# Folding a convolution's second transform stage into 64 by 64 products on sums and differences

## The chip, the cores and the metric

The kernel runs on one core of one Trainium2 chip. What counts is the device time of one execution in microseconds (us), as the median of several runs. The core has a matrix engine (PE, with its weight loads PEld), a vector engine (DVE), a scalar engine (ACT), GpSimd (POOL) and a sync engine (SP), which here only issues transfers. Each works through its own list of instructions in order; semaphores order them among each other. GpSimd and ACT issue some transfers too.

## The reference, cut to what matters

```python
def reference(u, A, B, C, log_dt, Dskip, x, w1, b1, w2, b2, gate_w):   # L = 2048, D = 512, N = 128
    g = sigmoid((u * gate_w).sum(-1, keepdims=True))
    dt = exp(log_dt)[:, None]
    P = exp((dt * A)[:, :, None] * arange(L))            # complex, A is D x N
    K = einsum("dn,dnl,dn->dl", C, P, dt * B).real       # 512 channels of 2048 taps
    a = irfft(rfft(pad(u.T)) * rfft(pad(K)))[:, :L].T + u * Dskip
    b = gelu(x @ w1 + b1) @ w2 + b2                      # 512 -> 1792 -> 512, 2048 rows
    return g * a + (1 - g) * b
```

All of it is float32. (In the reference's input list `x` of the dense branch is an input of its own.) The long convolution is done as a Fourier transform in two stages over a 32 by 64 split of the 2048 rows, a product of spectra, and the inverse in two stages.

## The kernel before, in words

**The front half** (`front`, about the first 398 us) holds four streams: the dense branch (`dense`: hidden products L917 to L919, output products L962 to L964, each product in three float32r pieces), the taps (`taps`: state powers on DVE, sines and exponentials on ACT, contraction over the state on PE at L726 for 16 chunks), the signal's transform (`signal`, 8 steps), and early loads. Each piece of work is a task with an engine, a duration and a due time. `Plan.run` walks through them with a clock of its own, takes on every engine the ready task with the least due time, and so fixes each engine's list. The constants at L34 to L86 are these due times and offsets. `vec`, `act`, `mm` and `move` make tasks for DVE, ACT, PE and the transfer queues.

**The first stage** (`first_stage`, L428 to L442) multiplies 32 rows of one residue group by a 32 by 64 matrix (`c1t`): four row groups of the array, two halves of its columns, into four PSUM banks. The signal's step feeds it two loaded tiles `ux`; the taps feed it the evacuated contraction of two chunks (`s1`, L744). Results go to DRAM as `tu_d` (signal, L459) and, through `sk`, as `tk_d` (taps, L767, eight stores per quarter of the channels). `tk_d` is complete only after the last chunk.

**The back half** (`conv`) holds 32 tiles of 128 rows by 512 channels (64 inputs of the second stage, real and imaginary parts below each other) and works in 16 turns `s` of two tiles:

- `pair(s, r, c, out)` is the second stage: for part c (real or imaginary) of the result and each of the two tiles, a product with 128 rows of contraction and 64 result rows (L1152). `signal(s)` makes two such parts into PSUM (`p2u`), `taps(s)` two more (`p2k`), which ACT copies to SBUF (`k`, L1160). The matrix for the second part is the first one with its halves exchanged and one sign turned; `matrices(m)` makes it (`f1`), on GpSimd for the first two groups of tiles (L1137, L1138), on ACT for the other six (L1140, L1141).
- `product(s)`: the complex product of spectra, six DVE operations of 512 elements (L1174 to L1179).
- `inverse(s)`: first stage back, four 64 by 64 products (L1191); `turn(s)`: ACT copies both results (`sa`, L1197), SP stores them to DRAM (`t4_d`, L1199), and after turns 3, 7, 11 and 15 the group of eight tiles is read back in another arrangement (L1214) into `t3` and `den`. GpSimd issues these group loads, except the last group's, which ACT issues.

The order inside a turn is: loads, `product(s)`, `signal(s+1)`, `taps(s+2)`, `inverse(s)`, `turn(s)`, `matrices`, loads of the dense result, and from turn 10 the gating of that result on ACT (L1234). PE's list in the back half is therefore inverse, signal, taps, inverse, and so on. After the turns PE does the dense products left over (`rest`, L1245), and then the last stage of the inverse (`pb`, L1316), which DVE, ACT and GpSimd gate and add (L1329 to L1332).

Of the kernel before, what the change touches and what calls it, by code (L numbers as in the profile page):

```python
# [17 lines left out]
P = 128  # L18
L = 2048
D = 512  # L20
# [13 lines left out]
T_0 = 28.031  # L34
T_MLP = 402.005
K_0 = 34.529
T_KG = 347.257
U_0 = 23
U_GAP = 18
LAG = 13.166  # L40
TABLE = 30.571
D_KA = -21.02
D_KP = -70.174
D_S1 = -64.005
D_EV = -0.687
D_H = -44.182
D_LO = -26.872
PS = (2, 3, 1, 2)
N_ACC, N_H, N_PK, N_PU = PS
D_SP = -0.459  # L50
MEM = (6, 2, 3)
N_LD, N_HL, N_ST = MEM
D_XS = -150.061
D_G = 2.936
N_WARM = 13
T_EARLY, T_LOFT, T_DEN = 434.731, 499.385, 583.061
Y_K, Y_U = 40.448, 33.741
W_MLP = (-0.0424, -0.0295, 0.0137)
W_KG = (-0.0358, -0.0266, -0.0229)
W_U = (-0.0255, -0.1355, -0.0209)  # L60
D_MAG = -1.089
D_ROT = 0.621
D_CON = -2.254
D_PHA = 0.57
D_PRE = -1.138
D_XL = 26
D_COE = -4.808
D_OUT = -10.383
D_DTB = -996.723
D_D0A = -269.982  # L70
D_LAST = -1.103
N_REST = 3
D_KA0 = 35
D_DT = 5
D_PRM = -94
D_D0 = 0
D_WAVE0 = -333.922
D_COE0 = -195.511
D_SP1 = -346.272
D_G0 = 14  # L80
D_GW = 568.694
D_XS0 = 115.71
T_PRE = 23
W_CAST = (0, 1, 0, 0, 1, 0, 1, 0, 1, 1, 0, 1, 0, 0)
X_CAST = (1, 1, 1, 1)
D_X0, D_B2, D_B2A, D_DM = -480, 20, -11.213, -79.268  # L86
# [23 lines left out]
def slot_q():  # L110
    return [32 + m if m < 32 else 63 - m for m in range(64)]
# [20 lines left out]
def constants():  # L132
# [8 lines left out]
    q = np.asarray(slot_q())  # L141
# [5 lines left out]
    c1 = np.tile(np.stack([er, ei], 2).reshape(32, 64), (4, 1))  # L147
# [23 lines left out]
    f2 = np.zeros((32, 2, 64, 64))  # L171
    g2 = np.zeros((32, 64, 32, 2))
    for n, k in enumerate(ko):
        er, ei = om(4 * np.outer(q - 31.5, k + 32 * k1) + (q - 31.5)[:, None])
        f2[n, 0], f2[n, 1] = er, -ei
# [135 lines left out]
def gated_mix(  # L311
# [34 lines left out]
    c1t = cp.tile([P, 64], F32, name="c1t")  # L346
# [6 lines left out]
    def front(pool, psum, keep, attic, loft, den):  # L353
# [46 lines left out]
        s1 = tiles(2, [P, D], "s1")  # L400

# [26 lines left out]
        def first_stage(xs, due, evac, ahead=2):  # L428
# [11 lines left out]
            mm(1.04, products, due + D_S1, [*(key for _, key in xs), "c1"], [key for _, key in banks], 0.5, 1.06, "f32")  # L440
            for r, (bank, key) in enumerate(banks):
                evac(r, bank, key)  # L442
# [3 lines left out]
        def signal():  # L446
            for s in range(8):
                t = U_0 + 16 * U_GAP * warp(s / 8, W_U)
                yield t + Y_U
                xs = [(ux[m], ("ux", m)) for m in range(2)]  # L450
                for m in range(2):
                    move(256, lambda m=m, s=s: nc.sync.dma_start(ux[m], xl[2 * s + m]), t - 10, [], [("ux", m)])

                def evac(r, pp, key, s=s, t=t):
                    k = take("st", N_ST)
                    act(512, lambda: nc.scalar.copy(st[k], pp), t + D_EV, [key], [("st", k)])
                    for m in range(2):
                        move(
                            128, lambda m=m: nc.sync.dma_start(rows[:, 8 * s + 4 * m + r], st[k][64 * m : 64 * m + 64]),  # L459
                            t, [("st", k)], [("u_d", 8 * s + 4 * m + r)], out=True,  # L460
                        )

                first_stage(xs, t, evac)
            yield None
# [251 lines left out]
        def contract(u, c, k, t):  # L716
# [28 lines left out]
            pair.append((xs, key))  # L745
# [13 lines left out]
            first_stage([pair.pop(0), pair.pop(0)], t, evac, 1 if g == 4 * NCH - 1 else 2)  # L759
# [350 lines left out]
    def conv(pool, ps, late, attic, loft, den):  # L1110
# [6 lines left out]
        c4s, mats, t2s = {}, {}, {}  # L1117

        def consts(m):
            cc = pool.tile([P, 384], F32, tag="cc", name=f"cc{m}", bufs=4)  # L1120
            nc.sync.dma_start(cc, c2[m])
            c4s[m] = cc
# [8 lines left out]
        def matrices(m):  # L1131

            cc = c4s[m]
            f = cc[:, 0:256].rearrange("p (n k) -> p n k", n=4)
            f1 = pool.tile([P, 4, 64], F32, tag="f1", name=f"f1{m}", bufs=2)
            if m < 2:
                nc.gpsimd.tensor_scalar(f1[0:64], f[64:128], -1.0, None, ALU.mult)  # L1137
                nc.gpsimd.tensor_copy(f1[64:128], f[0:64])  # L1138
            else:
                nc.scalar.mul(f1[0:64], f[64:128], -1.0)  # L1140
                nc.scalar.copy(f1[64:128], f[0:64])  # L1141
            mats[m] = (f, f1), cc[:, 256:384].rearrange("p (s k) -> p s k", s=2)

        fac, pus, prod, pas = {}, {}, {}, {}

        def pair(s, r, c, out):

            for i in range(2):
                n = 2 * s + i
                w = mats[n // 4][0][c][:, n % 4]  # L1150
                x = t2s[n] if r else us[n]
                nc.tensor.matmul(out[64 * i : 64 * i + 64], w, x, start=True, stop=True)  # L1152

        def taps(s):
            fac[s] = []
            for c in range(2):
                pk = ps.tile([P, D], F32, tag=f"pk{c}", name=f"p2k{s}{c}", bufs=1)
                pair(s, 1, c, pk)
                k = pool.tile([P, D], F32, tag=f"k{c}", name=f"k{s}{c}", bufs=2)
                nc.scalar.copy(k, pk)  # L1160
                fac[s].append(k)

        def signal(s):
            pus[s] = []
            for c in range(2):
                pu = ps.tile([P, D], F32, tag=f"pu{2 * (s % 2) + c}", name=f"p2u{s}{c}", bufs=1)
                pair(s, 0, c, pu)
                pus[s].append(pu)

        def product(s):  # L1170
# [3 lines left out]
            nc.vector.tensor_mul(v[0], ur, kr)  # L1174
            nc.vector.tensor_mul(v[1], ur, ki)
# [17 lines left out]
        def turn(s):  # L1193

            for n in (2 * s, 2 * s + 1):
# [8 lines left out]
                for h in (0, 4, 8, 16, 24) if g == 3 else (0, 8, 16, 24):  # L1204
# [9 lines left out]
                    on.dma_start(to, rows[:, h:e])  # L1214

        accs, mos = {}, {}
        held, after = [], []
# [40 lines left out]
        matrices(0)  # L1258
        matrices(1)
# [3 lines left out]
        for s in range(16):  # L1263
# [11 lines left out]
            product(s)  # L1275
            if s + 1 < 16:
                signal(s + 1)
# [9 lines left out]
            if s % 2 and s < 13:  # L1287
                matrices(s // 2 + 2)
# [133 lines left out]
```

## Time and profile before

| | us |
|---|---|
| runs | 508.63, 508.01, 507.02; median 508.01 |
| span of the profiled execution | 506.3 |
| what lies around the span (median less span) | 1.7 |
| PE busy / DVE / ACT / POOL in the span | 494.8 / 429.0 / 347.2 / 53.5 |
| share of all DMA engines' time on SP's queue | 53.7% |

Times in the profile are counted from the span's start. The profile shows no time of its own for the profiled execution, only its span; the median of the runs lies 1.7 us above it, and that is taken as what lies around a span. A busy PE in these rows is not a PE at its peak: matmuls overlap, and how far apart they start says more than how long each is shown. A float32 product appears as two records.

### The profile page before, as it was taken

Reading aid. Unit: us, or ns where it says so; the run is one execution under the profiler, and the core shown is the slowest. Engines: PE = TensorE matmul, PEld = TensorE weight load, DVE = VectorE, ACT = ScalarE, POOL = GpSimd, SP = SyncE. Lnnn points to the kernel's source line nnn. Section 1 sums busy time; section 2 is a strip of 40 time slices with the busy share of each in tenths; the row PEclk is TensorE's granted clock in tenths of the full one; section 3 lists DMA queues with packets and bytes.
Section 4 is the critical chain, followed back from the end, with each engine's and each line's share of the span. In section 5 each row is a group of like instructions: output and inputs, shape, how many; then the busy total and the mean of one; then the engine's idle time right before and its main releaser. Section 6 shows DMA issues by size and latency. Waiting matters only on the chain.

```text
span 506.3 us, 12185 instructions
## 1 busy us (share of the span) xinstructions
PE 494.8 (98%) x4798; PEld 380.3 (75%) x4798; DVE 429.0 (85%) x794; ACT 347.2 (69%) x625; POOL 53.5 (11%) x93
## 2 busy tenths in 40 slices
PE   7999999999999999999999999999999999999995
PEld 7886988998889889889789878989889722222551
DVE  6999999998999999999899989999921188877544
ACT  4898757699683889968487997657643445568513
POOL 1001010101002011011110012001010300020003
PEclk9999999999999999999999999999999999999998
DMA  8958896416788545889850276984588997999998
GB/s 288 381 178 235 298 296 219 84 65 200 182 239 222 156 147 126 262 187 238 201 128 2 84 167 156 208 266 104 189 208 180 282 390 266 336 374 382 320 321 312
DMA packets 82680, 112.32 MB, mean 222 GB/s; under 512 B 39644, under 2 KB 41184, under 8 KB 82080
## 3 DMA queue, kind: packets, MB, share of 16 engines
q1 hardware_dynamic: 74704, 87.06, 53.7%
q0 software_dynamic: 7264, 21.73, 18.3%
q10 hardware_dynamic: 656, 2.75, 1.7%
q8 instruction: 38, 0.62, 0.5%
q14 instruction: 18, 0.15, 0.1%
HBM read 61.71 MB, written 49.81 MB: 220 GB/s over the span
## 4 chain that ended last, share of the span: by engine, by line
PE 70%; DVE 13%; DMA 7%; ACT 4%; SPq 2%; issue 2%; DVEq 0%; ACTq 0%
PE pk L726 10%; PE acc L962 7%; PE ph L917 7%; PE ph L919 7%; PE ph L918 7%; PE acc L964 7%; PE acc L963 6%; PE p2u L1152 5%; PE p2k L1152 4%; PE pa L1191 3%; PE pb L1316 3%; DMA tk<-tk_d 2%; PE ph L438 2%; DVE y L689 2%; SPq L767 2%
## 5 line engine op out<-in xcount | busy, mean ns | idle before, releaser
L917 PE MATMUL ph<-xh,wh 128*128 128x256 f32 x448 | 127.7, 285 | 2.2 <-ACT wh L826 1.6
L919 PE MATMUL ph<-xh,wl 128*128 128x256 f32 x448 | 127.1, 284 | 0.4 <-DVE wl L828 0.4
L918 PE MATMUL ph<-xlo,wh 128*128 128x256 f32 x448 | 126.7, 283 | 0.0
L917 PEld LDWEIGHTS ph<-xh,wh 128*128 128x128 f32 x448 | 85.2, 190 | 9.5 <-issue 5.0
L918 PEld LDWEIGHTS ph<-xlo,wh 128*128 128x128 f32 x448 | 85.1, 190 | 1.8
L919 PEld LDWEIGHTS ph<-xh,wl 128*128 128x128 f32 x448 | 85.1, 190 | 1.0 <-DVE wl L828 1.0
L962 PE MATMUL acc<-wh,hh 128*128 128x512 f32 x206 | 83.2, 404 | 0.1
L964 PE MATMUL acc<-wh,hl 128*128 128x512 f32 x206 | 80.9, 393 | 0.5 <-DVE hl L947 0.5
L963 PE MATMUL acc<-wl,hh 128*128 128x512 f32 x206 | 80.9, 393 | 0.0
L934 ACT ACTIVATE ph<-ph,b1t 128x256 f32<-128x256 f32 x112 | 50.4, 450 | 43.6 <-PE ph L919 41.8
L726 PE MATMUL pk<-y,den 128*32 128x64 f32 x2048 | 61.4, 290 | 0.0
L726 PEld LDWEIGHTS pk<-y,den 128*32 128x32 f32 x2048 | 57.2, 136 | 3.5 <-issue 1.4
L962 PEld LDWEIGHTS acc<-wh,hh 128*128 128x128 f32 x206 | 38.7, 188 | 17.8 <-issue 7.4
L947 DVE TENSOR_TENSOR hl<-ph,hh 128x512 fp32r<-128x512 f32 (+1 forms) x62 | 38.4, 620 | 14.9 <-ACT hh L937 14.6
L689 DVE TENSOR_TENSOR y<-y,ea 128x64 f32<-128x64 f32 (+4 forms) x80 | 45.5, 569 | 2.1 <-ACT y L679 1.5
L964 PEld LDWEIGHTS acc<-wh,hl 128*128 128x128 f32 x206 | 38.7, 188 | 10.3 <-DVE hl L947 1.7
L963 PEld LDWEIGHTS acc<-wl,hh 128*128 128x128 f32 x206 | 38.7, 188 | 6.2
L937 ACT CAST hh<-ph 128x512 fp32r<-128x512 f32 (+1 forms) x62 | 33.0, 533 | 9.4 <-PE acc L963 6.2
L532 DVE TENSOR_TENSOR loft<-den,zz 128x256 f32<-128x256 f32 (+2 forms) x48 | 37.4, 779 | 0.7
L533 DVE TENSOR_TENSOR loft<-den,zz 128x256 f32<-128x256 f32 (+2 forms) x48 | 37.3, 777 | 0.0
L701 DVE TENSOR_TENSOR y<-y,loft 128x2048 f32<-128x2048 f32 x16 | 36.6, 2288 | 0.6 <-ACT loft L650 0.5
L1160 ACT COPY k<-p2k 128x512 f32<-128x512 f32 x32 | 18.5, 585 | 23.8 <-PE p2k L1152 8.0
(190 smaller groups left out, 876.0 us busy)
## 6 DMA issues: line engine op xcount, KB each, us to landing
tu_d<-attic SPq DMA_DIRECT2D x64, 128.0 KB, 3.9
tk_d<-sk SPq DMA_DIRECT2D x32, 256.0 KB, 5.3
t_d<-sa SPq DMA_DIRECT2D x32, 256.0 KB, 5.4
tk<-tk_d SPq DMA_DIRECT2D x24, 256.0 KB, 5.1
attic<-in_xt_dram SPq DMA_DIRECT2D x16, 256.0 KB, 5.1
xh_d<-xh SPq DMA_DIRECT2D x8, 512.0 KB, 5.0
xl_d<-xlo SPq DMA_DIRECT2D x8, 512.0 KB, 4.6
attic<-in_xs_dram SPq DMA_DIRECT2D x16, 256.0 KB, 4.9
```

Of the source, the lines that this page charges most:

```text
L532: vec(2 * m, lambda: vv.tensor_mul(t, a, br), due, [ka, *kb], [kt])
L689: nc.vector.tensor_mul(both(n, 64 - 3 * n, n), both(0, 64 - n, n), an)
L726: nc.tensor.matmul(pks[q][32 * j : 32 * j + 32, :, gg], x[:, r, :, ch], y[:, r, :, ch], start=(r == 0), stop=(r == 1), skip_group_check=True,)
L917: nc.tensor.matmul(p, h, xh[xk][:, d], start=(d == 0), stop=False)
L918: nc.tensor.matmul(p, h, xlo[xk][:, d], start=False, stop=False)
L919: nc.tensor.matmul(p, lo, xh[xk][:, d], start=False, stop=(d == 3))
L934: nc.scalar.activation(phs[q][:, n], phs[q][:, n], AF.Gelu_apprx_tanh, bias=b1t[:, f : f + 1])
L947: nc.vector.tensor_sub(lo, phs[q][:, 0:nf], hi.bitcast(F32))
L962: nc.tensor.matmul(a, h, wh[1][w], start=start, stop=False)
L963: nc.tensor.matmul(a, h, wl[1][w], start=False, stop=False)
L964: nc.tensor.matmul(a, l, wh[1][w], start=False, stop=(j == 3))
L1152: nc.tensor.matmul(out[64 * i : 64 * i + 64], w, x, start=True, stop=True)
```

## The change

1. **Inputs of the second stage as sums and differences.** Rows of the signal that lie mirrored are added and subtracted by GpSimd before the first stage (two operations of 512 elements per step); for the taps the two halves of `s1` are (two operations of 256 elements per chunk, the difference into a new tile `sd`). The first stage multiplies sums with the old matrix and differences with a second one beside it (`c1t` is 128 columns wide now); for the taps each product is split into two of half the width.
2. **The second stage as 64 by 64 products.** One part of the result needs the sums alone, the other the differences alone, so each product contracts over 64 rows instead of 128. `pair` makes four products on four quarters of the array. The second matrix, `matrices` and its ACT and GpSimd instructions are gone.
3. **In the loop** the subtraction of the complex product moves from DVE to GpSimd, right after the two products that feed it; and the group loads that `turn` gave to GpSimd at once are kept in `behind` and issued after the next turn's `product`.
4. The table of due times is another one, GpSimd's operations are tasks of the plan (`pool_op`), and the scratch for GpSimd's transfers is set to 8192.

The diff, cut to its core (of the table, three rows):

```diff
-T_KG = 347.257
+T_KG = 351.021
-D_S1 = -64.005
+D_S1 = -105.306
+D_UD = -20.4
...
+    sums, differences = np.stack([er, ei], 2), np.stack([ei, -er], 2)
+    c1 = np.tile(np.concatenate([sums.reshape(32, 64), differences.reshape(32, 64)], 1), (4, 1))
...
+        f2[n, :, 0] = np.cos(np.outer(m + 0.5, a))
+        f2[n, :, 1] = np.sin(np.outer(m + 0.5, a))
...
+        def pool_op(n, fn, due, reads=(), writes=()):
+            return pl.add("GP", 0.18 + n / 470.0, fn, due, reads, writes)
...
-                    for m, (x, _) in enumerate(xs):
-                        nc.tensor.matmul(bank[64 * m : 64 * m + 64], c1t[rs], x[rs], start=True, stop=True)
+                    for m, parts in enumerate(xs):
+                        ms = slice(64 * m, 64 * m + 64)
+                        for x, at, sign in parts:
+                            c = c1t[rs, 64 * sign : 64 * sign + 64]
+                            nc.tensor.matmul(bank[ms, at], c, x[rs], start=True, stop=True)
...
+                pool_op(512, lambda: nc.gpsimd.tensor_sub(ud, ux[0], ux[1]), t + D_UD, [("ux", 0), ("ux", 1)], ["ud"])
+                pool_op(512, lambda: nc.gpsimd.tensor_add(ux[0], ux[0], ux[1]), t + D_UD, [("ux", 1)], [("ux", 0)])
...
-            pair.append((xs, key))
+            low, high, df = xs[:, 0 : D // 2], xs[:, D // 2 : D], sd[c % 2]
+            pool_op(256, lambda: nc.gpsimd.tensor_sub(df, low, high), t + D_S1, [key], [("sd", c % 2)])
+            pool_op(256, lambda: nc.gpsimd.tensor_add(low, low, high), t + D_S1, [], [key])
+            pair.append([(low, slice(0, D // 2), 0), (df, slice(D // 2, D), 1)])
...
-        def pair(s, r, c, out):
-            for i in range(2):
-                n = 2 * s + i
-                w = mats[n // 4][0][c][:, n % 4]
-                x = t2s[n] if r else us[n]
-                nc.tensor.matmul(out[64 * i : 64 * i + 64], w, x, start=True, stop=True)
+        def pair(s, r, outs):
+            for c in range(2):
+                rows = slice(64 * c, 64 * c + 64)
+                for i in range(2):
+                    n = 2 * s + i
+                    w = mats[n // 4][0][rows, n % 4]
+                    x = (t2s[n] if r else us[n])[rows]
+                    nc.tensor.matmul(outs[c][64 * i : 64 * i + 64], w, x, start=True, stop=True)
...
             nc.vector.tensor_mul(v[0], ur, kr)
+            nc.vector.tensor_mul(zs[0], ui, ki)
+            nc.gpsimd.tensor_sub(v[0], v[0], zs[0])
             nc.vector.tensor_mul(v[1], ur, ki)
-            nc.vector.tensor_mul(zs[0], ui, ki)
             nc.vector.tensor_mul(zs[1], ui, kr)
-            nc.vector.tensor_sub(v[0], v[0], zs[0])
             nc.vector.tensor_add(v[1], v[1], zs[1])
...
-                    on = nc.gpsimd if n < 31 else nc.scalar
...
-                    on.dma_start(to, rows[:, h:e])
+                    if n < 31:
+                        behind.append((to, rows[:, h:e]))
+                        continue
+                    nc.scalar.dma_start(to, rows[:, h:e])
...
             product(s)
+            for to, rows in behind:
+                nc.gpsimd.dma_start(to, rows)
+            behind.clear()
...
-            if s % 2 and s < 13:
-                matrices(s // 2 + 2)
```

Three places show how instructions are moved. In these rows a name is a tile, with its line in the kernel before or in the changed one.

The first is GpSimd's list in the back half (`t` and `den` are filled by group loads, `v` and `z` belong to the product of spectra). Before, from the first matrix to the held loads of turn 9:

```order
L1138 COPY f_4786<-cc_4759 64x256
L1137 TENSOR_SCALAR f_4789<-cc_4767 64x256
L1138 COPY f_4789<-cc_4767 64x256
L1214 DMA den<-t_d 32x4096
L1214 DMA t_4765<-t_d 32x4096 x2
L1214 DMA den<-t_d 32x4096
L1214 DMA t_4765<-t_d 32x4096 x2
L1282 DMA t_4765<-t_d 32x4096 x2
```

Changed, from turn 4 to turn 9:

```order
L1186 TENSOR_TENSOR v_5101<-v_5101,z_4872 128x512
L1287 DMA den<-t_d 32x4096
L1287 DMA t_4880<-t_d 32x4096 x2
L1186 TENSOR_TENSOR v_5144<-v_5144,z_4872 128x512
L1186 TENSOR_TENSOR v_5185<-v_5185,z_4872 128x512
L1186 TENSOR_TENSOR v_5219<-v_5219,z_4872 128x512
L1186 TENSOR_TENSOR v_5256<-v_5256,z_4872 128x512
L1287 DMA den<-t_d 32x4096
L1287 DMA t_4880<-t_d 32x4096 x2
L1186 TENSOR_TENSOR v_5294<-v_5294,z_4872 128x512
L1295 DMA t_4880<-t_d 32x4096 x2
```

GpSimd had nothing but loads there; now one subtraction of every turn is in its list, and the group loads of turn 3 stand between the subtractions of turns 4 and 5, those of turn 7 between 8 and 9.

The second is DVE's list for one turn of the loop, before and changed:

```order
L1174 TENSOR_TENSOR v_5041<-p2u_5009,k_4970 128x512
L1175 TENSOR_TENSOR v_5042<-p2u_5009,k_4975 128x512
L1176 TENSOR_TENSOR z_4757<-p2u_5012,k_4975 128x512
L1177 TENSOR_TENSOR z_4758<-p2u_5012,k_4970 128x512
L1178 TENSOR_TENSOR v_5041<-v_5041,z_4757 128x512
L1179 TENSOR_TENSOR v_5042<-v_5042,z_4758 128x512
```

```order
L1184 TENSOR_TENSOR v_5144<-p2u_5112,k_5079 128x512
L1185 TENSOR_TENSOR z_4872<-p2u_5113,k_5081 128x512
L1187 TENSOR_TENSOR v_5145<-p2u_5112,k_5081 128x512
L1188 TENSOR_TENSOR z_4873<-p2u_5113,k_5079 128x512
L1189 TENSOR_TENSOR v_5145<-v_5145,z_4873 128x512
```

Five operations stand where six stood, and only the last of them takes both operands from SBUF.

The third is GpSimd's list late in the front half, between two reloads of the dense branch's input (`xh`, `xlo`). Before and changed:

```order
L848 DMA xh_105<-xh_d 128x1024
L848 DMA xlo_107<-xl_d 128x1024
L1006 DMA out_dram<-io_143 128x512
L678 MEMSET y 128x32
L1006 DMA out_dram<-io_144 128x512
```

```order
L759 TENSOR_TENSOR sd_105<-s_103 128x256
L867 DMA xh_108<-xh_d 128x1024
L760 TENSOR_TENSOR s_103<-s_103 128x256
L867 DMA xlo_110<-xl_d 128x1024
L1025 DMA out_dram<-io_146 128x512
L462 TENSOR_TENSOR ud<-attic,ux_102 128x512
L463 TENSOR_TENSOR attic<-attic,ux_102 128x512
L1025 DMA out_dram<-io_147 128x512
L691 MEMSET y 128x32
```

Sums and differences for PE's first stage stand now in the same list as the reloads and the accumulating stores, one of them behind a reload. On PE, 96 hidden products and 30 output products stand between the last first stage of the taps and the second stage; before there were 120 and 30.

More of the change, by code (lines that the diff above doesn't have):

```diff
@@ L400, in front @@
         s1 = tiles(2, [P, D], "s1")
+        sd = tiles(2, [P, D // 2], "sd")
+        ud = pool.tile([P, D], F32, name="ud")
         xh, xlo = (
@@ L426, in front, with first_stage @@
         step = [0]
-        def first_stage(xs, due, evac, ahead=2):
+        def first_stage(xs, keys, due, evac, ahead=2, hold=1.04):
             q = (step[0] + ahead) % N_H
@@ L757, in evac @@
                 )
-            first_stage([pair.pop(0), pair.pop(0)], t, evac, 1 if g == 4 * NCH - 1 else 2)
+            first_stage(
+                [pair.pop(0), pair.pop(0)], [(z, m) for z in ("s1", "sd") for m in range(2)], t, evac,
+                1 if g == 4 * NCH - 1 else 2, 1.1,
+            )
             if c < NCH - 1:
@@ L1116, in conv @@
         ko = k0_order()
[L1117 removed]
+        mats, t2s = {}, {}
         def consts(m):
@@ L1163, in signal @@
         def signal(s):
[L1164 to L1168, printed above, removed]
+            pus[s] = [
+                ps.tile([P, D], F32, tag=f"pu{2 * (s % 2) + c}", name=f"p2u{s}{c}", bufs=1) for c in range(2)
+            ]
+            pair(s, 0, pus[s])
         def product(s):
```

131 lines of the change are left out of this document (59 added, 72 removed).

## The prediction

> **What bounds the kernel now.** I read the page first, then the chain of waits, then each engine's timeline in the back half, and the windows for what is full.
>
> ```profile
> span 506.3 us, 12185 instructions
> PE 494.8 (98%) x4798; PEld 380.3 (75%) x4798; DVE 429.0 (85%) x794; ACT 347.2 (69%) x625; POOL 53.5 (11%) x93
> ```
>
> The median of the runs shown is 508.0, so 1.7 us lie around this span; I add them back at the end. PE looks full everywhere, so the stages have to be told apart. In the back half the chain (start, length, engine, tile) runs on PE alone:
>
> ```profile
> 408.91 1.69 PE pa L1191 x8
> ...
> 414.18 1.02 PE pa L1191 x8
> 415.19 1.87 PE p2u L1152 x8
> 417.06 1.72 PE p2k L1152 x8
> 418.78 1.02 PE pa L1191 x8
> ...
> 472.30 1.02 PE pa L1191 x8
> 475.60 1.02 PE pa L1191 x8
> 476.62 0.43 PE acc L1245
> 487.04 13.91 PE pb L1316 x68
> ```
>
> A turn is 1.02 (inverse) + 1.87 (signal) + 1.72 (taps) = 4.61 us, and nothing else ends it. From the first inverse to the last are 475.60 - 408.91 = 66.7 us; the 30.7 us behind the last are leftover dense products, the last stage and the final stores, which the change leaves alone. The windows (time, then PE, PEld, DVE, ACT, POOL busy with counts, granted clock, DMA share, GB/s) show what is next in line:
>
> ```profile
> 408.90:476.60 67.70, 67.69 (x354) 19.43 (x354) 55.57 (x91) 42.82 (x80) 5.36 (x10) 1.00 0.95 344
> 461.20:465.80 4.60, 4.60 (x30) 1.26 (x26) 3.66 (x7) 4.18 (x8) 0.00 (x0) 1.00 1.05 405
> ```
>
> The transfers are almost as full as PE: 344 GB/s on average, about 405 where they are pressed. The loop moves 67.7 x 344 = 23.3 MB, which at 405 takes 57.5 us. No loop with these bytes goes below that. In the front half DVE is as full as PE: 310 of 320 us.
>
> ```profile
> 40.00:360.00 320.00, 310.02 (x580) 1.00 0.66 178
> ```
>
> **The change, part by part.**
>
> *Second stages.* A pair of them is now four products of 64 by 64, the form of the inverse, which takes 1.02 where the 128-row form takes 1.72 to 1.87. Signal's extra 0.15 I keep: a PE turn of 3 x 1.02 + 0.15 = 3.2 us instead of 4.6. It pays only if the other engines follow. DVE in one turn before (start, length, then idle before it in brackets):
>
> ```profile
> 443.94 0.69 DVE L1174 TENSOR_TENSOR v<-p2u,k 128x512 f32<-128x512 f32 x1 [0.92 <-ACT sa L1197]
> ...
> 446.94 0.69 DVE L1179 TENSOR_TENSOR v<-v,z 128x512 f32<-128x512 f32 x1
> ...
> 448.54 0.69 DVE L1174 TENSOR_TENSOR v<-p2u,k 128x512 f32<-128x512 f32 x1 [0.92 <-ACT sa L1197]
> ```
>
> Starts are 0.60 apart, five operations are 3.0: DVE keeps a 3.2 turn, just. With six it would not (3.6); that is what the move to GpSimd buys. ACT, in a turn with gating:
>
> ```profile
> 456.68 1.07 ACT L1197 COPY sa<-pa 128x512 f32<-128x512 f32 x2 [0.39 <-PE pa L1191]
> 457.64 1.34 ACT L1234 ACTIVATE attic<-attic,gate 128x512 f32<-128x512 f32 x2
> 459.47 0.59 ACT L1160 COPY k<-p2k 128x512 f32<-128x512 f32 x1 [0.48 <-ACT attic L1234]
> 460.31 0.59 ACT L1160 COPY k<-p2k 128x512 f32<-128x512 f32 x1 [0.26 <-PE p2k L1152]
> ```
>
> 1.07 + 2 x 0.59 = 2.25 without gating; with it 3.6. So turns 1 to 9 take 3.2, turns 10 to 14 take 3.6 (ACT), and the last keeps its 3.3 (475.60 less 472.30). The sum is 28.8 + 18.0 + 3.3 = 50.1, or 16.6 less than 66.7. The removed matrix copies on ACT were off the path: nothing.
>
> *GpSimd's subtraction and the group loads.* The nearest row is GpSimd's addition of the same shape at the end of the kernel:
>
> ```profile
> L1330 POOL TENSOR_TENSOR loft<-loft,sa 128x512 f32<-128x512 f32 x2 | 2.5, 1271 | 22.9 <-DMA t<-t_d 22.5 <-ACT sa L1329 0.4
> ```
>
> 1.27 us start after two DVE products (1.2) and are over at 2.5, before DVE's fifth operation at 3.0: by itself free. The price is the queue. The inverse needs this result, and a group load at the head of GpSimd's list waits until the turn's stores have landed. When that was (inverse, then the loads it led to):
>
> ```profile
> 423.38 1.02 PE pa L1191 x8
> ...
> 441.80 1.02 PE pa L1191 x8
> ...
> 460.21 1.02 PE pa L1191 x8
> ```
>
> ```profile
> 430.43 1.09 POOL L1214 DMA_DIRECT2D t<-t_d  x2
> ...
> 451.09 1.05 POOL L1214 DMA_DIRECT2D t<-t_d  x2
> ...
> 469.36 0.53 POOL L1214 DMA_DIRECT2D t<-t_d  x1
> ```
>
> Issuing ended 8.1, 10.3 and 9.7 us after the inverses of turns 3, 7 and 11 had begun. The subtraction of turns 5, 9 and 13 stands behind it, so these inverses cannot begin before 9.4, 11.6 and 11.0 us; two turns of 3.2 or 3.6 would have had them at 6.4, 6.4 and 7.2. The stalls are 3.0, 5.2 and 3.8, together 12.0 us, and everything behind on PE, ACT and SP waits with them. The bounds are nothing (stores that land in time) and, were each landing 2 us later in the fuller queue, 18. I take 12.0. The held loads of turn 9 find their data long stored and cost 1 us of GpSimd's slack. The loop comes to 50.1 + 12.0 = 62.1, above the transfers' 57.5, so bytes set no second bound.
>
> *The start.* The tap stream gets two GpSimd operations per chunk, some 1.3 us together if half the width costs half. At the last chunk they are covered by dense products that stand there; but the last first stage now has 24 products fewer behind it:
>
> ```profile
> 379.72 0.28 PE L918 MATMUL ph<-xlo,wh 128*128 128x256 f32 x1
> 379.84 0.28 PE L919 MATMUL ph<-xh,wl 128*128 128x256 f32 x1
> ...
> 406.61 1.37 PE L1152 MATMUL p2k<-tk,f 128*64 128x512 f32 x3
> ```
>
> 24 x 0.12 = 2.9 us later are the last `tk_d` stores and so the loads of `tk`; taps(2) got its last tile before 406.6 and would get it before 409.5. Against that, the first product of spectra no longer stands behind an accumulating store:
>
> ```profile
> 406.37 0.69 DVE L1175 TENSOR_TENSOR v<-p2u,k 128x512 f32<-128x512 f32 x1 [1.95 <-DMA out_dram<-io]
> ```
>
> From there five more DVE operations led to 408.91; now these are done early and the first inverse follows taps(2) directly. I take +0.6, with bounds of -1.5 (loads no later) and +3. On SP the loop's list keeps its order; one early load instead of three stands between the last tap stores and the `tk` loads, but these wait for the stores' landing anyway: nothing. The first stages' split products keep their columns; sums and differences of the signal are made ahead of need. Both I cost at nothing, under dense products of PE; if that cover is gone, a step waits up to 2.5 us.
>
> *Clock.* After a stall PE may come back slower. The trace has one idle PE, at the end:
>
> ```profile
> 502.00:506.00 4.00, 0.00 (x0) 0.00 (x0) 0.00 (x0) 0.00 (x0) 0.00 (x0) 0.62 0.61 224
> ```
>
> Within 4 us the granted clock falls. Bounds: nothing, or one turn of PE again for each of three stalls, 9.6. I take 0.5, near the lower end, since two stalls are short. [...]
>
> **The sum.** 506.3 + 0.6 - 16.6 + 12.0 + 0.5 = 502.8 us of span, **504.5 us** with the 1.7 around it, 0.7% below 508.0. Of this kernel's measurement about 0.3% (1.5 us) can be told from no change.
>
> **The rivals.**
>
> *Stores land in time.* In the loop now, landings are fastest where the queue is short. If the group loads find their data, the loop is bound by the bytes: 57.5 instead of 62.1, and the time is **500**. For it: between stalls nothing else is late. Against it: two of three groups waited over 7 us even in the slower loop.
>
> *The stalls eat the gain.* With transfers pressed from start to end each store lands later, and PE loses clock: each group's stores landing another 1.2 us later than counted give 504.5 + 3.6 = **508**, no change. For it speaks the 0.95 share; against it, that PE's stalls themselves let the queue run empty.
>
> *Second stages don't overlap* by quarters: turns stay 4.6, the stalls shrink to what exceeds 9.2 us (0.2 + 2.4 + 1.8), and the time is 508.0 + 0.6 + 4.4 = **513**. Against it: the inverse row, in this very form.
>
> *GpSimd stops DVE in the front half.* This is the one that ends slower. DVE's work there is mostly on two SBUF operands, a small part reads PSUM:
>
> ```profile
> L701 DVE TENSOR_TENSOR y<-y,loft 128x2048 f32<-128x2048 f32 x16 | 36.6, 2288 | 0.6 <-ACT loft L650 0.5
> L947 DVE TENSOR_TENSOR hl<-ph,hh 128x512 fp32r<-128x512 f32 x42 | 28.9, 689 | 4.9 <-ACT hh L937 4.8
> L947 DVE TENSOR_TENSOR hl<-ph,hh 128x256 fp32r<-128x256 f32 x14 | 5.9, 421 | 0.1
> ```
>
> The two forms of L947 are 34.8 of the 310 us, 11%; nearly all else is of the first kind. GpSimd gets 16 operations of 1.27 and 32 of half that, 41 us. If a GpSimd operation that reads SBUF holds up a DVE operation with two SBUF operands, DVE loses up to 0.89 x 41 = 36 us, has 10 us of idle time to absorb it, and the tap stream, with the loop behind it, comes 26 us later: **530**. It decides from the point where more than 13.5 us of DVE are lost (10 idle, 3.5 gained), that is a bit over a third of it; half of it gives 512.5. No row of this trace has the two side by side: GpSimd's additions at the end run beside DVE operations that read PSUM, and stay at 1.27. [...]
>
> **How the numbers follow.** Chances: forecast 0.40, stores in time 0.16, gain eaten 0.14, no overlap 0.04, DVE held up 0.26. [...] Faster by over 0.3%: 0.9 x 0.40 + 0.16 + 0.01 = 0.53. Within: 0.04 + 0.11 = 0.15. Slower: 0.26 + 0.04 + 0.02 = 0.32. The forecast's own range is 501 to 508 (stalls of 9 to 15 us, start from -1.5 to +3). The full range is 498 to 518: it takes in the byte bound below, and above the half-strength hold-up, leaving out the strongest.
>
> **What would show it.** L1163 pairs at about 1.02 us and DVE five operations 0.60 apart would show the loop's terms; inverses of turns 5, 9 and 13 that wait for POOL L1186, with group loads ahead of it, the stalls; a first inverse near 409.5 the start. In the front half, L701 at 2.29 us and L532 unchanged beside POOL L759 would rule out the hold-up; DVE operations stretched or spaced by GpSimd's, and a tap stream ending much later than 377, would make the prediction wrong.

## The result, and the profile after

The changed kernel takes 530.9 us where the kernel before takes 507.8: 1.046 times as long (95% interval 1.043 to 1.049). The profiled execution took 530.6 us with a span of 528.6, so 2.0 lie around it. One of the four runs took 538.6 us, at a lower granted clock (0.954, the others 0.968 to 0.978), and is left out of the ratio. The page of the changed kernel begins so; the third row is the head of its chain of waits, by engine:

```profile
span 528.6 us, 12495 instructions
PE 484.7 (92%) x4926; PEld 386.8 (73%) x4926; DVE 448.0 (85%) x778; ACT 343.9 (65%) x616; POOL 134.7 (25%) x153
DVE 44%; PE 31%; DMA 9%; issue 7%; ACT 4%; POOL 3%; SPq 2%; DVEq 0%; POOLq 0%; ACTq 0%
```

In the kernel before PE was busy 98% of the time. Now it is 92%, and DVE carries the longest part of the chain. DVE has 16 instructions fewer (778 against 794) and yet 19.0 us more busy time. The window of the front half shows the same thing from another side (columns as before):

```profile
40.00:360.00 320.00, 306.70 (x3433) 262.45 (x3432) 312.87 (x543) 231.66 (x410) 83.53 (x93) 0.99 0.64 168
```

DVE is as full as before (312.9 of 320 us, then 310.0), but gets 543 operations done where it did 580. Its groups, shapes kept apart, say which ones take longer (count, then busy us and mean ns). L702, L714 and L966 are the L689, L701 and L947 of the kernel before:

```profile
L702 DVE TENSOR_TENSOR y<-y,ea 128x64 f32<-128x64 f32 x16 | 6.7, 420 | 0.0
L702 DVE TENSOR_TENSOR y<-y,ea 128x128 f32<-128x128 f32 x16 | 8.1, 509 | 0.1
L702 DVE TENSOR_TENSOR y<-y,ea 128x256 f32<-128x256 f32 x16 | 9.2, 578 | 0.1
L966 DVE TENSOR_TENSOR hl<-ph,hh 128x512 fp32r<-128x512 f32 x46 | 31.3, 681 | 14.1 <-ACT hh L956 14.1
L714 DVE TENSOR_TENSOR y<-y,loft 128x2048 f32<-128x2048 f32 x16 | 36.5, 2279 | 0.0
```

The first three were 221, 288 and 422 ns. L966, which reads PSUM (`ph`), is unchanged (689 before). So is L714, although both its inputs lie in SBUF; only one of its 16 operations lies beside one of GpSimd's new ones. GpSimd's new operations are stretched as well:

```profile
L760 POOL TENSOR_TENSOR s<-s 128x256 f32<-128x256 f32 x16 | 20.1, 1255 | 0.9
L759 POOL TENSOR_TENSOR sd<-s 128x256 f32<-128x256 f32 x16 | 16.6, 1041 | 39.6 <-ACT s L757 39.6
L462 POOL TENSOR_TENSOR ud<-attic,ux 128x512 f32<-128x512 f32 x8 | 14.7, 1834 | 51.6 <-DMA attic<-in_xl_dram 29.1 <-issue 11.9 <-DMA ux<-in_xl_dram 10.1
L1186 POOL TENSOR_TENSOR v<-v,z 128x512 f32<-128x512 f32 x16 | 20.5, 1280 | 29.4 <-DVE z L1185 29.3
```

In the loop, where DVE mostly reads PSUM, the 512-wide one takes 1.28 us; in the front half the same shape takes 1.83. The 256-wide one takes 0.74 where DVE leaves it alone, as behind the last contraction:

```profile
400.52 0.74 POOL L759 TENSOR_TENSOR sd<-s 128x256 f32<-128x256 f32 x1 [5.62 <-ACT s L757]
```

One place of the front half shows both sides. First GpSimd's timeline there, then DVE's (start, length):

```profile
80.08 3.85 POOL L462 TENSOR_TENSOR ud<-attic,ux 128x512 f32<-128x512 f32 x1 [6.90 <-DMA attic<-in_xl_dram]
84.01 1.64 POOL L463 TENSOR_TENSOR attic<-attic,ux 128x512 f32<-128x512 f32 x1
```

```profile
80.01 1.21 DVE L721 SCALAR_TENSOR_TENSOR y<-y,loft 128x1024 f32<-128x1024 f32 x1
81.14 0.28 DVE L547 TENSOR_TENSOR den<-loft 128x128 f32<-128x128 f32 x1
81.34 1.21 DVE L725 TENSOR_TENSOR y<-y,loft 128x1024 f32<-128x1024 f32 x1
82.48 0.28 DVE L548 TENSOR_TENSOR den<-loft 128x128 f32<-128x128 f32 x1
82.68 0.41 DVE L966 TENSOR_TENSOR hl<-ph,hh 128x256 fp32r<-128x256 f32 x1
83.02 1.46 DVE L545 TENSOR_TENSOR loft<-den,zz 128x512 f32<-128x512 f32 x1
84.40 1.80 DVE L546 TENSOR_TENSOR loft<-den,zz 128x512 f32<-128x512 f32 x1
```

GpSimd's subtraction starts at 80.08 while DVE runs one operation with two SBUF inputs after another, and gets nowhere: it ends at 83.93, 1.25 us after DVE came to L966, which has a PSUM input (82.68). L545 starts at 83.02, still beside the subtraction, and takes 1.46 us instead of 0.69: it ends about 0.55 after the subtraction does. Then L546 starts beside GpSimd's addition and takes 1.80. By these starts and ends each side stands still while the other works.

The loop is the other half of the story. PE's inverses (turns 0, 3, 5, 7, 9, 11, 13 and 15; idle time before in brackets):

```profile
430.70 0.59 PE L1201 MATMUL pa<-v,cc 64*64 64x512 f32 x1
439.03 1.21 PE L1201 MATMUL pa<-v,cc 64*64 64x512 f32 x5
454.26 1.98 PE L1201 MATMUL pa<-v,cc 64*64 64x512 f32 x8 [7.09 <-POOL v L1186]
460.85 1.20 PE L1201 MATMUL pa<-v,cc 64*64 64x512 f32 x8
472.23 1.99 PE L1201 MATMUL pa<-v,cc 64*64 64x512 f32 x8 [5.35 <-POOL v L1186]
480.06 1.03 PE L1201 MATMUL pa<-v,cc 64*64 64x512 f32 x8
491.27 1.98 PE L1201 MATMUL pa<-v,cc 64*64 64x512 f32 x8 [5.00 <-POOL v L1186]
497.92 1.44 PE L1201 MATMUL pa<-v,cc 64*64 64x512 f32 x8
```

The first inverse comes at 430.7 instead of 408.9: the front half is 21.8 us late. From the first to the last are 67.2 us, and were 66.7. Behind the last are 30.7, as before. So nearly all of the loss (21.8 of 22.3 us of span) is in the front half, and the loop has gained nothing.

### The profile page after: what moved, and what is told of

It is laid out like the page before. It is cut to its first block, busy times and chain, and to the rows that moved or that the text cites. A ratio compares the mean times of both kernels' runs of the same rounds, so it can differ in the third digit from the quotient of the medians.

```text
span 528.6 us, 12495 instructions
## 1 busy us (share of the span) xinstructions
PE 484.7 (92%) x4926; PEld 386.8 (73%) x4926; DVE 448.0 (85%) x778; ACT 343.9 (65%) x616; POOL 134.7 (25%) x153
## 4 chain that ended last, share of the span: by engine, by line
DVE 44%; PE 31%; DMA 9%; issue 7%; ACT 4%; POOL 3%; SPq 2%; DVEq 0%; POOLq 0%; ACTq 0%
DVE y L702 6%; DVE loft L546 5%; DVE loft L545 4%; PE pk L739 4%; DVE y L714 4%; DVE hl L966 3%; PE pa L1201 3%; PE pb L1327 3%; DMA t_d<-sa 3%; DVE den L547 2%; PE ph L936 2%; PE ph L938 2%; PE ph L937 2%; PE acc L981 2%; DVE phase L644 2%
## 5 line engine op out<-in xcount | busy, mean ns | idle before, releaser
L702 DVE TENSOR_TENSOR y<-y,ea 128x64 f32<-128x64 f32 (+4 forms) x80 | 55.0, 687 | 0.5
L966 DVE TENSOR_TENSOR hl<-ph,hh 128x512 fp32r<-128x512 f32 (+1 forms) x62 | 37.9, 612 | 19.7 <-ACT hh L956 19.7
L981 PEld LDWEIGHTS acc<-wh,hh 128*128 128x128 f32 x206 | 39.1, 190 | 17.3 <-issue 6.6
L546 DVE TENSOR_TENSOR loft<-den,zz 128x256 f32<-128x256 f32 (+2 forms) x48 | 40.9, 853 | 0.0
L545 DVE TENSOR_TENSOR loft<-den,zz 128x256 f32<-128x256 f32 (+2 forms) x48 | 40.3, 841 | 0.5
L1201 PE MATMUL pa<-v,cc 64*64 64x512 f32 x128 | 23.8, 693 | 17.4 <-POOL v L1186 17.4
L714 DVE TENSOR_TENSOR y<-y,loft 128x2048 f32<-128x2048 f32 x16 | 36.5, 2279 | 0.0
```

The costliest lines, as they stand in the source:

```text
L545: vec(2 * m, lambda: vv.tensor_mul(t, a, br), due, [ka, *kb], [kt])
L546: vec(2 * m, lambda: vv.tensor_mul(v, a, bi), due, [ka, *kb], [kv])
L702: nc.vector.tensor_mul(both(n, 64 - 3 * n, n), both(0, 64 - n, n), an)
L714: v.tensor_mul(y[:, 0].rearrange("p (a b) c -> p a b c", a=2), e.rearrange("p (a b) c -> p a b c", a=2), cc,)
L966: nc.vector.tensor_sub(lo, phs[q][:, 0:nf], hi.bitcast(F32))
L981: nc.tensor.matmul(a, h, wh[1][w], start=start, stop=False)
```

## The experiments

The theory after the result: GpSimd operations that read SBUF and DVE operations with two SBUF inputs shut each other out, and the 48 sums and differences cost the front half its 22 us. Rivals: the new table of due times makes the front half long; or the first stages wait for GpSimd's results. For the loop: the stalls come from GpSimd's list, or from the bytes. In each group below the kernel before ran beside the others, at 507.2 to 507.9 us.

### What made the front half late

**The sums and differences left out.** They stay tasks of the plan, so no other engine's list changes:

```diff
-lambda: nc.gpsimd.tensor_sub(ud, ux[0], ux[1])
+lambda: None
... (the other three likewise; ud and sd are zeroed once)
```

> Left out: the 48 sums and differences of GpSimd in the front half (the products then run on unsummed and zeroed inputs). Everything else of the changed kernel stays, every other engine's list included. Theory (GpSimd's reads and DVE's two-input operations shut each other out): the first inverse, 430.7 us with them, comes back to about 409, and the time from 530.6 to 508 to 511. Rival (the new table of due times is what makes the front half long): 522 to 531.

Measured: 507.1 us, 1.000 of the kernel before (0.999 to 1.002), first inverse at 407.9. The table is not the cause. All 23.8 us between the change and this kernel belong to these 48 operations. It also shows what the rest of the change is worth: nothing.

**Memsets in their place.**

```diff
-lambda: nc.gpsimd.tensor_sub(ud, ux[0], ux[1])
+lambda: [nc.gpsimd.memset(ud, 0.0) for _ in range(2)]
... (the other three likewise)
```

> Left out: the same 48 sums and differences; in the place of each stand two memsets of the same tile on GpSimd, so that GpSimd is about as long busy, the first stages still wait for it, but it reads nothing from SBUF. Theory (the hold-up is one of reads): DVE's 128x64 operations on y are back at about 0.22 us (0.43 in the changed kernel), the time is that without the operations, 508 to 512. Rival (the first stages wait for GpSimd's results, or its queue is too long): 522 to 531.

Measured: 509.9 us (1.005, 1.003 to 1.008). The memsets' and DVE's groups in this kernel:

```profile
L462 POOL MEMSET ud<- 128x512 f32 x16 | 9.5, 596 | 20.0 <-PE pu L448 19.6
L760 POOL MEMSET s<- 128x256 f32 x32 | 11.4, 355 | 16.2 <-ACT s L757 15.2
L702 DVE TENSOR_TENSOR y<-y,ea 128x64 f32<-128x64 f32 x16 | 3.5, 219 | 0.4 <-ACT y L692 0.2
```

GpSimd is busy with 96 memsets of 0.35 to 0.60 us, 40.6 us in all, the first stages still wait for those on their inputs, and DVE's small operations are back at 219 ns. So about 2.8 us (509.9 less 507.1) are waits for a GpSimd that is busy as long without reading, or for its queue. The rest hangs on GpSimd reading SBUF.

**The operations alone, in the kernel before.** 48 subtractions of the same widths, whose results nobody reads; the lists of PE, DVE, ACT and SP are those of the kernel before, row by row (the scratch for GpSimd's transfers is 8192, as in the change, to make room for the new tiles):

```diff
+                for _ in range(2):
+                    pool_op(512, lambda: nc.gpsimd.tensor_sub(ud, ux[0], ux[1]), t - 20.4, [("ux", 0), ("ux", 1)], ["ud"])
...
+            for _ in range(2):
+                pool_op(256, lambda: nc.gpsimd.tensor_sub(df, low, high), t + D_S1, [key], [("sd", c % 2)])
```

> The kernel before, with 48 GpSimd subtractions added in the front half, as many and as wide as in the change, at the same places of the streams; they read the signal's loads and the evacuated contractions and write to tiles that nobody reads. The lists of PE, DVE, ACT and SP are unchanged. Theory (shutting out): DVE's 128x64 operations on y stretch from 0.22 to about 0.4 us, the first inverse comes some 20 us later, 524 to 534. Rivals (table, or waits for GpSimd's results): nobody waits for these operations, 507 to 511.

Measured: 527.6 us (1.041, 1.037 to 1.045), first inverse at 428.9. Page and groups:

```profile
PE 501.3 (95%) x4798; PEld 378.8 (72%) x4798; DVE 459.5 (87%) x794; ACT 348.2 (66%) x625; POOL 117.6 (22%) x141
L697 DVE TENSOR_TENSOR y<-y,ea 128x64 f32<-128x64 f32 x16 | 7.1, 445 | 0.4 <-ACT y L687 0.4
L958 DVE TENSOR_TENSOR hl<-ph,hh 128x512 fp32r<-128x512 f32 x46 | 31.3, 680 | 11.5 <-ACT hh L948 11.5
```

The same 794 DVE instructions take 459.5 us instead of 429.0. No engine computes anything from GpSimd's results here. Together the three runs show the cause: it is not the table and not the waits, but GpSimd's reads beside DVE's reads.

**Copies instead of subtractions.** The same, with two copies for each subtraction, one of each input:

```diff
-lambda: nc.gpsimd.tensor_sub(ud, ux[0], ux[1])
+lambda: [nc.gpsimd.tensor_copy(ud, ux[m]) for m in range(2)]
... (the 256-wide ones likewise, of low and high)
```

> The kernel before, with 96 GpSimd copies in the places where the 48 idle subtractions stood, two for one (each of the subtraction's inputs copied once), again into tiles that nobody reads. A copy has one input; a 64x256 copy took 0.39 us in the kernel before, so the dose is some 45 to 50 us, like the subtractions'. Theory (any GpSimd operation that reads SBUF shuts out DVE's two-input ones): 522 to 530, small DVE operations stretched as by the subtractions. Rival (only operations with two inputs on both engines meet): 507 to 511, DVE's 128x64 on y at 0.22.

Measured: 516.4 us (1.019, 1.016 to 1.022), between both forecasts.

```profile
PE 498.8 (97%) x4798; PEld 378.6 (73%) x4798; DVE 449.0 (87%) x794; ACT 348.2 (67%) x625; POOL 135.6 (26%) x189
L697 DVE TENSOR_TENSOR y<-y,ea 128x64 f32<-128x64 f32 x16 | 5.4, 338 | 0.4 <-ACT y L687 0.4
```

The rival falls: operations with one input hold DVE up too (338 ns, 20.0 us of DVE in all). They cost less than the subtractions (30.5), though not because they are shorter. Four of the 256-wide copies found DVE idle and took 0.40 us each:

```profile
385.78 1.79 POOL L755 COPY sd<-s 128x256 f32<-128x256 f32 x4 [4.19 <-ACT s L752]
```

The shortest 512-wide one took 0.62. By these the 96 copies are 45 us long unhindered, and the 48 subtractions, by 1.28 and 0.74, are 44. So a copy costs DVE about two thirds of what a subtraction of the same length does; why is not settled.

**Half of the operations.** The change with the taps' 32 left out, and the change with the signal's 16 left out (edits as in the first run, here for the signal's alone):

```diff
-pool_op(256, lambda: nc.gpsimd.tensor_sub(df, low, high), ...
+pool_op(256, lambda: None, ...
... (the addition likewise; sd is zeroed once)
```

> Left out: the taps' 32 sums and differences; the signal's 16 of 512 elements stay (about 22 of the 45 us that GpSimd's 48 take unhindered). If DVE first uses up its idle time (10 us) before the front half gets longer: 0.68 us of DVE per us of GpSimd (30.5 over 45, as the idle subtractions showed) make 15, less 10, so 511 to 514. If every us counts from the first: half of 23.8, 517 to 521. If the taps' operations alone matter, since they stand ahead of DVE's chain of powers: 507 to 509.

> Left out: the signal's 16 sums and differences; the taps' 32 of 256 elements stay (about 23 of the 45 us). By idle time used up first: 512 to 515; by every us counted: 517 to 521; if the taps' alone matter: 528 to 531.

Measured: 518.2 us with the signal's alone (1.023, 1.020 to 1.025), 520.1 with the taps' alone (1.025, 1.022 to 1.029). That is 11.1 and 13.0 above the 507.1 without any, together 24.1, and all 48 cost 23.8. So the cost starts with the first operations; nothing near the 10 us of DVE's idle time is used up before. DVE's busy time rises too: 435.9 and 433.8 against 420.6, 15.3 and 13.2 more.

**The same operations on DVE.**

```diff
-pool_op(512, lambda: nc.gpsimd.tensor_sub(ud, ux[0], ux[1]), ...
+vec(512, lambda: nc.vector.tensor_sub(ud, ux[0], ux[1]), ...
... (the other three likewise)
```

> The changed kernel with the 48 sums and differences of the front half on DVE, as tasks of the plan there; the loop as in the change. Theory (shutting out): DVE does in 16 x 0.60 + 32 x 0.34 = 20.5 us what costs it 30 us when GpSimd does it, of which some 10 were absorbed; the time is 10 to 15 above that without the operations: 517 to 522, better than the change's 530.9. Rival (the front is long because DVE and PE have no room for anything, whoever does the sums): 528 to 533.

Measured: 522.0 us (1.029, 1.025 to 1.032), at the upper end of what was expected. That is 14.9 above none at all, where GpSimd costs 23.8. DVE's busy time is 17.3 above that without the operations (437.9 against 420.6), where it was 27.4. The engine that was to be relieved does the work itself for less than it loses beside the helper. (With tasks on DVE the plan lays out the other engines' lists anew too; what that is worth was not measured by itself.)

### What the loop waits for

**The subtraction on DVE.**

```diff
-            nc.gpsimd.tensor_sub(v[0], v[0], zs[0])
+            nc.vector.tensor_sub(v[0], v[0], zs[0])
```

> The changed kernel with the loop's subtraction on DVE again; the group loads stay on GpSimd, behind the next product. Theory (the inverses wait because the subtraction stands behind group loads in GpSimd's list): six DVE operations at 0.60 make turns of 3.6, first to last inverse falls from 67.3 to 57 to 60, the time to 520 to 523.5. Rival (the loop is bound by its bytes: 24.4 MB at the 392 GB/s of its fullest stretch are 62 us, and waits for landings take the place of the one removed): 62 to 67 from first to last inverse, 525 to 531.

Measured: 526.1 us (1.037, 1.034 to 1.040), 4.8 less than the change, and 63.1 from first to last inverse (432.1 to 495.2). Both lie in the rival's ranges (525 to 531, 62 to 67), near their lower ends: the loop got 4.1 us shorter (67.2 before the edit), and PE now waits 6.3 us in three places for ACT's copies `sa`. So the list and something else bind. The same edit without the late front half (the 48 operations left out as in the first run):

> Left out: the 48 sums and differences of the front half; and the loop's subtraction is on DVE. What the change could bring at most if its sums were free, with this loop. Theory (queue order and bytes both bind the loop): as far below 507.1 as the same edit brought behind the late front, 501 to 504. Rival (GpSimd's list alone binds it): 16 turns of 3.85, first to last inverse 57.8, 495 to 498. Rival (bytes alone): 505 to 508.

Measured: 502.0 us (0.990, 0.987 to 0.993), the time that was expected of both causes. PE's inverses there, from two turns:

```profile
412.26 0.65 PE L1204 MATMUL pa<-v,cc 64*64 64x512 f32 x3 [0.79 <-DVE v L1192]
416.11 0.65 PE L1204 MATMUL pa<-v,cc 64*64 64x512 f32 x3 [0.79 <-DVE v L1192]
```

Turns are 3.85 apart and end in DVE's sixth operation; first to last inverse takes 60.0 (407.5 to 467.5). The loop by itself is nearer the forecast of the list alone (57.8). That the time is above the 495 to 498 of that forecast comes to 2.2 from the loop and to 2.0 from behind the last inverse (32.2 us follow it, 30.2 without this edit). The 502.0 are also the best that this change can reach with this loop, if its sums cost nothing: 1% below the kernel before.

**Fewer bytes**, on top of it: the loads of the last signal tiles and of the dense result for six turns left out. By the pages that is 4.5 MB of the kernel's (107.91 against 112.37): five signal tiles, not the twelve that the expectation counts.

```diff
-                nc.sync.dma_start(us[n], tu_d[ko[n]])
+                pass
...
-                dense(HERE[s - 7], nc.sync)
+                dense(HERE[s - 7], None)
```

> Left out: the 48 sums and differences, and in the loop the loads of the last signal tiles and of the dense result for six turns (12 of 0.26 and 6 of 0.52 MB, 6.3 of 24.4 MB); the subtraction is on DVE. Theory (bytes bind what is left above the DVE turns): turns of 3.85 all through, first to last inverse 57.8 to 59, 495 to 498. Rival (bytes don't matter): the time of the version with all its transfers, 501 to 504.

Measured: 500.1 us (0.986, 0.983 to 0.989), between the forecasts. First to last inverse is 57.7, as forecast (15 turns of 3.85), so these loads held 2.3 us of the 60.0 in this pair of runs. But the first inverse came at 410.1, 2.6 later than with all transfers, though nothing before it was edited; why is not settled.

**Subtraction on GpSimd, group loads one more turn later.**

```diff
-                        behind.append((to, rows[:, h:e]))
+                        behind.append((s + 2, to, rows[:, h:e]))
...
-            for to, rows in behind:
+            while behind and behind[0][0] <= s:
+                _, to, rows = behind.pop(0)
                 nc.gpsimd.dma_start(to, rows)
```

> Left out: the 48 sums and differences of the front half. The loop's subtraction stays on GpSimd, but each group's loads are issued one more turn later, when their stores should have landed. Theory (both bind): the three stalls of 5 to 7 us shrink, but the 24.4 MB at 392 to 407 GB/s take 60 to 62 us, so first to last inverse goes from 68 to 60 to 63 and the time to 499 to 503. Rival (GpSimd's list alone binds): turns of 3.12 and 3.6, 50 to 52 from first to last, 489 to 492. Rival (bytes alone): 505 to 508.

Measured: 506.2 us (0.998, 0.996 to 1.001), above what was expected; 64.6 from first to last inverse, where 68.2 go by without the edit. Two of its inverses:

```profile
430.85 1.67 PE L1204 MATMUL pa<-v,cc 64*64 64x512 f32 x8 [4.15 <-POOL v L1189]
451.77 1.99 PE L1204 MATMUL pa<-v,cc 64*64 64x512 f32 x8 [6.87 <-POOL v L1189]
```

The stalls remain. The window of this loop (granted clock, DMA share and GB/s at the end):

```profile
408.00:468.00 60.00, 43.30 (x342) 17.66 (x334) 43.92 (x71) 33.92 (x64) 23.27 (x24) 0.91 1.04 385
```

The transfers are full, and the loads still find the stores not landed when GpSimd comes to them a turn later. The first load of each group goes 11.4, 12.6 and 9.0 us after the inverse of turns 3, 7 and 11 began; without the edit it went after 11.1, 7.2 and 10.1. How much of the 64.6 is bytes and how much the wait in GpSimd's list was not taken apart further.

**Both edits that need no left-out work**, sums on DVE and the loop's subtraction on DVE:

```diff
-pool_op(512, lambda: nc.gpsimd.tensor_sub(ud, ux[0], ux[1]), ...
+vec(512, lambda: nc.vector.tensor_sub(ud, ux[0], ux[1]), ...
...
-            nc.gpsimd.tensor_sub(v[0], v[0], zs[0])
+            nc.vector.tensor_sub(v[0], v[0], zs[0])
```

> Nothing left out: sums and differences on DVE in the front half, and the loop's subtraction on DVE; GpSimd only issues the group loads. The two gains add up if they have separate causes: 522.0 less the 4.8 to 5.1 that the loop's edit brought behind a late and behind an early front: 516 to 518. If the front's lateness hid part of the loop's waits: 518 to 521.

Measured: 515.9 us (1.018, 1.016 to 1.021). The gains add up (522.0 less 515.9 is 6.1). It is the best full version of these edits and still slower than the kernel before. No full version beat that kernel. The loop of this version is that of the 526.1 and the 502.0, with the same bytes, and takes 58.4 us from first to last inverse where they take 63.1 and 60.0. So the loop's time also depends on how the front half ends, and of the 2.3 us put down to bytes above only 0.7 remain by this run; why was not settled.

## Why the prediction was wrong

It said 504.5 and the time is 530.9, outside the range. What happened is the rival that it put at 530 with a chance of 0.26.

- **The failing step** is the sentence that costs the first stages' split products and the signal's sums and differences "at nothing, under dense products of PE", together with the taps' two operations per chunk, said to be covered. PE's cover was there. But these operations do not run beside PE's work only; they run beside DVE's, DVE was full, and they held it up. The 48 operations cost 23.8 us.
- **The rival's own numbers.** The full price was put at 36 us of DVE, 0.89 of GpSimd's time; the change loses 27.4 (448.0 less 420.6 without the operations), 0.62 of 44. Of that, 10 us of idle time were to be absorbed, with effects only from 13.5 us on. In the change hardly any is: 27.4 lost, 23.8 late, and half doses cost their share. In the kernel before, 30.5 us lost made 20.4 late and 20.0 made 9.1, so there the 10 were absorbed. So the loss was put 8.6 too high, what is absorbed 6.4 too high, and the time without the operations 2.6 too low. That these cancel, and the 530 lies so near the 530.9, is luck; the mechanism is right. Why the changed order has no slack for it was not tested.
- **Why it got too small a chance.** That part of the work is small was, in the author's estimate, a reason against it. The rows show the opposite. In the front half of the change 38 of DVE's operations take over 60 ns longer than the same form took before, 29.0 us together, and 19.0 of these fall on operations of at most 256 elements. L714 with its 2.28 us was spared because GpSimd's operations hardly met it; beside the copies its like (L709) was stretched:

```profile
75.82 2.69 DVE L709 TENSOR_TENSOR y<-y,loft 128x2048 f32<-128x2048 f32 x1
```

- **Second stages: right.** A pair is 0.86 apart from the next (inverse to inverse 2.57 in the shortest turn), shorter than the forecast 1.02. DVE's five operations come every 3.12 us, forecast 3.0: the fifth, which has two SBUF inputs, starts 0.72 after the fourth, beside GpSimd's subtraction.
- **Stalls: right in place, one mis-sized.** The inverses of turns 5, 9 and 13 wait for L1186 behind group loads, as said. From turn 7 to 9 and 11 to 13 pass 11.4 and 11.2 us, forecast 11.6 and 11.0. From turn 3 to 5 pass 15.2, forecast 9.4: that term is 5.8 too small. The chain of waits of the changed kernel at this place (its longer pieces; others are left out):

```profile
436.30 5.28 DMA t_d<-sa
441.65 0.58 ACT sa L1207
...
445.43 5.30 DMA t_d<-sa
...
451.29 0.56 POOL den L1287
451.84 1.07 POOL t L1287 x2
452.93 1.29 POOL v L1186
454.26 1.98 PE pa L1201 x8
```

ACT's first copy at 441.65 waits until an earlier store of the same ring of six `sa` tiles has landed, at 441.58. The second copy is over at 442.87, its store is issued only at 445.43, behind SP's other issues, and lands 5.30 later; then go the group loads, and behind them the subtraction. In the kernel before, the last store of turn 3 was issued 2.3 us after the inverse had begun (423.38) and landed 3.4 later; here it is 6.4 and 5.3. So about 4 us of the difference are a store that is issued late, and about 2 a slower landing. The forecast took both from the slower loop, with its turns of 4.6 us.

- **Clock: too small.** 0.5 was taken. The granted clock (third number from the end) falls with the stalls:

```profile
430.70:445.00 14.30, 12.90 (x111) 6.46 (x107) 14.16 (x24) 8.56 (x17) 5.11 (x4) 1.00 1.05 392
445.00:455.00 10.00, 2.91 (x26) 0.86 (x20) 2.18 (x5) 3.08 (x6) 2.94 (x4) 0.76 1.06 376
474.00:484.00 10.00, 10.00 (x81) 4.07 (x76) 8.67 (x15) 7.34 (x14) 3.06 (x3) 0.82 0.99 379
```

After the three stalls, of 7.1, 5.4 and 5.0 us, the inverse takes 1.98 to 1.99 instead of 1.02, and the next turns come 4.0, 5.2 and 3.4 later, forecast 3.2, 3.6 and 3.6: some 2 us.
- **Loop in sum:** 67.2 against 62.6 forecast with the clock. The transfers' floor of 57.5 was not tested: the shortest loop with all its bytes took 58.4, and the 57.7 with bytes taken out is DVE's 15 turns of 3.85.
- **Start and tail: right, apart from the operations.** Without them the first inverse comes 1.0 earlier than before (forecast +0.6, bounds -1.5 to +3); behind the last inverse nothing changed.

So even without the hold-up the forecast would have been 2.6 us too low (507.1): that part is its rival "the stalls eat the gain", at 508.

## What to carry to other kernels

Before work goes to GpSimd, look at what DVE does in the same stretch: if DVE is full there with operations on two SBUF inputs, a GpSimd operation that reads SBUF can hold DVE up. Here the 48 took 27.4 to 30.5 us from DVE, about two thirds of their own 44 us. GpSimd is also slower for the same shape (0.74 us for 256 elements, where DVE starts one every 0.33), so DVE did the work for less itself. GpSimd cost little where it only wrote (about 2.8 us for 96 memsets), and nothing that shows where DVE read PSUM (DVE's operations beside the loop's subtraction stay at 0.68 us). And do not put a result that PE waits for behind an instruction of the same list that waits for a transfer: three inverses of the changed kernel waited 5.0 to 7.1 us so, and issuing the transfer a turn later took only 3.6 off the loop's 68.2 us here, since what it waits for came, on the whole, no sooner.

## What the runs showed of the hardware that was not expected

- The hold-up is no sharing of speed. At 80.08 GpSimd's operation waits through DVE's back-to-back two-input operations (3.85 us, of which only the last 1.25 are its own), and DVE's next one of that kind (L545, 1.46 us instead of 0.69) then waits for GpSimd's end. Memsets, which only write, left DVE's 128x64 operations on y at 219 ns, where they take 218 without the 48 operations.
- A waiting operation can be passed over: in four places of the front half (GpSimd's operations at 80.08, 230.11, 323.57 and 368.10, which take 2.55 to 3.88 us) three to five further DVE operations start before GpSimd gets in, there at one that reads PSUM. But of the 25 others that took over 0.1 us longer than 0.74 or 1.28 us, 23 got in before any further DVE operation started, also between two that read SBUF alone, and the second of them pays:

```profile
71.93 1.25 POOL L760 TENSOR_TENSOR s<-s 128x256 f32<-128x256 f32 x1
```

```profile
71.38 1.21 DVE L546 TENSOR_TENSOR loft<-den,zz 128x1024 f32<-128x1024 f32 x1
72.51 0.82 DVE L702 TENSOR_TENSOR y<-y,ea 128x128 f32<-128x128 f32 x1
```

  GpSimd's 0.74 us here end at 73.18, so they began at about 72.44, as L546 was ending; L702 takes 0.82 instead of 0.29. Of the 38 stretched operations only 5 stand right behind one that reads PSUM. What decides whether GpSimd gets in is not settled.
- A GpSimd copy with one SBUF input holds DVE up as well (128x64 from 221 to 338 ns).
- How much lateness is absorbed could not be read from DVE's idle time. Without the 48 operations it is busy for 310 of 320 us in both orders of work, yet 30.5 us lost made 20.4 late in the one and 27.4 made 23.8 in the other. What sets it was not tested.
